# A last tile multiplied by a nested seven-product form: one core, RetNet attention and a SwiGLU block

## The chip, the cores and the metric

The kernel runs on one core of a Trainium2 chip, in float32. The metric is the device time of one execution in microseconds (us). "Before" is the kernel without the change, "after" the kernel with it. Engines are named as in the profile: PE (TensorE), DVE (VectorE), ACT (ScalarE), POOL (GpSimd), SP (SyncE). PSUM banks named bankA, bankB, bankC, bankE, inner and outer are the places that PE writes to.

## The reference

```python
def _attn_ref(q, k, v):                        # 8 x 8 x 576 x 64
    scores = np.matmul(q, k.transpose(0, 1, 3, 2)) / np.sqrt(64)
    gamma = 1.0 - 2.0 ** (-5.0 - np.arange(8))
    rel = pos[:, None] - pos[None, :]
    Dmat = np.where(rel >= 0, gamma[:, None, None] ** rel[None], 0.0)
    return np.matmul(scores * Dmat[None], v)   # no softmax

x = attn.transpose(0, 2, 1, 3).reshape(4608, 512)
g, val = x @ w_gate, x @ w_val                 # 512 -> 1536
out = (g / (1 + np.exp(-g)) * val) @ w_out     # 1536 -> 512
```

The inputs are drawn from normal distributions; nothing in them is sparse.

## The kernel before

**Tiles.** The tokens are worked on in five tiles: tile 0 has 512 tokens and is multiplied in the plain way, tiles 1 to 4 have 1024 each. Every tile has an up stage (x to hidden) and then a down stage (hidden to output). The attention that makes x for a coming tile is cut into "ticks" and mixed among the steps of tiles 1 to 3 (`merge`, L1202); tile 4 has no ticks. The order of all engines' instructions is the order of the program text: each engine has one stream and works through it in order, and so do SP's and ACT's DMA issues, which stand in these streams and wait there for what they need.

**Up stage of tiles 1 to 4.** d_ff is worked on in three quarters of 512 (`NQ` = 3, so named in the code). In each, x (512 x 1024) times the two weight pieces (512 x 512 of gate and value) is computed by a form with 26 products (table `UP`, `N` = 26) in place of the plain number. `up_step` (L1108) is one product: 4 matmuls of 128 x 128 x 256 at L1124 into one bank, two for gate and two for value. `reads` (L1048) then takes the bank away: ACT's copy (L1058), sums with further partial results on DVE or POOL (L1061), and for a finished block ACT's silu (L1145) and the product with the value half (L1148 to L1152), which writes `hid`. Four banks are used in turn, so PE can be four products ahead of what empties them.

**Operands.** The x operands are sums of x blocks (`x_sums`). The weight operands are sums of weight blocks, made once, in tile 1 (`w_sums`, on POOL), and stored to DRAM: `up_ops` on ACT's queue (L1128), `dn_ops` on SP's (L978). From tile 2 on SP fetches them again (L1022) into a ring of eight slots; `fetch()` is called once a step, so the fetch is up to eight steps ahead of its use.

**Down stage.** `down_step` (L1162) is one of 26 products with 6 matmuls (L1173). Its operands are sums of hidden blocks (L1165), its results leave by SP (L1182). In the last four or so steps the first x sums of the next tile are made on DVE.

**Memory.** `arena` holds `hid` (three quarters, 4096 words a partition each), and behind it the up weights of tile 1, whose place later serves as the ring (`ring`). `rest` holds x of the even tiles, partial results (`part`), x sums and hidden sums. `x_odd` holds x of the odd tiles.

Of the kernel before, what the change touches and what calls it, by code (L numbers as in the profile page):

```python
# [12 lines left out]
F32 = mybir.dt.float32  # L13
# [4 lines left out]
ALU = mybir.AluOpType  # L18
# [117 lines left out]

def terms(text):

    return [t.split() for t in text.split(",") if t.strip()]
# [16 lines left out]
def kernel(  # L156
# [83 lines left out]
    ring = arena[:, 4 * QW + 2560 - 8 * 768 :].rearrange("p (s x) -> p s x", x=768)  # L240
# [672 lines left out]
    dn_ops = [dr.tile([P, 768], F32, name=f"dn{i}") for i in range(N)]  # L913

# [96 lines left out]
    fetches = [("dn", 1, i) for i in range(N)]  # L1011
    for n in range(2, NTILE):
        fetches += [("up", qd, i) for qd in range(NQ) for i in range(N)] + [("dn", n, i) for i in range(N)]
    fetched = [0]
    turn = [5, 4, 1, 6, 7, 2, 0, 3]

    def fetch():
        m = fetched[0]
        if m < len(fetches):
            what, a, i = fetches[m]  # L1020
            src = up_ops[a][i] if what == "up" else dn_ops[i]
            nc.sync.dma_start(out=ring[:, turn[m % 8], 0 : src.shape[-1]], in_=src)  # L1022
            fetched[0] += 1

    used = [0]

    def operand():
        m = used[0]
        used[0] += 1
        return ring[:, turn[m % 8]]  # L1030
# [77 lines left out]
    def up_step(n, qd, i):  # L1108
# [5 lines left out]
        if busy:  # L1114
            if i > 1:
                w_sums(qd, i)
            w = up_view(qd)(wslot)
        else:
            w = operand()[:, 0:512].rearrange("p (g x) -> p g x", g=2)
# [7 lines left out]
        if busy:  # L1127
            nc.scalar.dma_start(out=up_ops[qd][i].rearrange("p (g x) -> p g x", g=2), in_=w)  # L1128
            if i in (20, 23) and qd + 1 < NQ:
                first_sums(qd + 1, *((0, 2) if i == 20 else (2, 4)))  # L1130
# [5 lines left out]
            if qd + 1 == NQ:  # L1136
                for _ in range({21: 3, 22: 2, N - 1: 3}.get(i, 0)):
                    fetch()
# [23 lines left out]
    def down_step(n, i):  # L1162
        label, opens, slot, hops, ops = down[i]
        for op in hops:
            add(nc.gpsimd if i % 3 == 1 and op[0] != "nad" else nc.vector, op, hid_view)  # L1165
        w = operand().rearrange("p (q x) -> p q x", q=NQ)
# [30 lines left out]
        if 0 <= at < X_FIRST and n + 1 < NTILE:  # L1197
            x_sums(n + 1, at, at + 2, True)
        go_on(3)


# [91 lines left out]
    for n in range(1, NTILE):  # L1293
        upto = needed(n + 1) if n + 1 < NTILE else done
        cut = (done + upto + (n == 1) * 2) // 2
        ups = [lambda qd=qd, i=i: up_step(n, qd, i) for qd in range(NQ) for i in range(N)]
# [49 lines left out]
```

## Time and profile before

| | before |
|---|---|
| runs, us | 1040.68, 1040.79, 1042.05 (median 1040.79) |
| span of the profiled execution (first to last instruction), us | 1037.2 |
| its own time beside the span | no single time is recorded for it; the median of the runs is 3.6 us above its span |
| mean granted clock of PE | 0.998 |
| busy: PE / DVE / ACT / POOL | 99% / 61% / 29% / 40% of the span |
| DMA | 199.12 MB, mean 192 GB/s |
| last up stage, us from the start | 831.5 to 966.3 |

A row of a profile's group has: source line, engine, operation, output <- inputs with shapes, count, then busy us in all and mean ns of one, then idle us of the engine just before and what ended it. A row of a timeline has: start, length in us, engine, line, operation. PE shows two MATMUL records for each f32 matmul of 128 x 128 x 256, so a step of four matmuls counts as x8.

### The profile page before, as it was taken

The page shows a single profiled execution, that of the slowest core. Times are in us where ns is not written, and L with a number is a line of the kernel's source. Part 1 is how long each engine was busy: PE and PEld are TensorE (multiplying, and loading weights), DVE is VectorE, ACT ScalarE, POOL GpSimd, SP SyncE. Part 2 cuts the span into 40 slices and gives each one's busy share as a digit, 9 for nine tenths or more (in the row PEclk, how much of TensorE's full clock was granted, in tenths as well). Part 3 has the DMA queues.
Part 4 walks back from the last instruction along what each step waited for, and adds up shares of the span by engine and source line. Part 5 has one row for each costly group of instructions (what it writes and reads, how often), then busy time and mean ns, then how long its engine had stood idle before and what let it go on. Part 6 is the DMA issues. An engine that isn't in the chain of part 4 may idle for free.

```text
span 1037.2 us, 21564 instructions
## 1 busy us (share of the span) xinstructions
PE 1023.1 (99%) x8440; PEld 846.0 (82%) x8440; DVE 633.2 (61%) x1070; ACT 299.6 (29%) x653; POOL 419.9 (40%) x369
## 2 busy tenths in 40 slices
PE   6999999999999999999999999999999999999998
PEld 5654555888888888888888888888888888888887
DVE  4488878676768667446458685435465644344644
ACT  3566433253544222222322103223211022231110
POOL 3401265867564236522134057222242583222425
PEclk9999999999999999999999999999999999999999
DMA  9999877777679887674686686555554465555653
GB/s 240 258 279 263 200 218 269 204 205 191 196 194 265 211 244 220 177 197 133 188 231 173 176 208 208 153 142 153 159 171 148 143 196 153 153 153 160 182 163 100
DMA packets 307244, 199.12 MB, mean 192 GB/s; under 512 B 215944, under 2 KB 251784, under 8 KB 307144
## 3 DMA queue, kind: packets, MB, share of 16 engines
q1 hardware_dynamic: 275720, 161.17, 58.2%
q10 hardware_dynamic: 30784, 36.18, 10.4%
q8 instruction: 67, 1.10, 0.5%
q0 software_dynamic: 640, 0.39, 0.2%
q14 instruction: 33, 0.27, 0.1%
HBM read 157.58 MB, written 40.11 MB: 191 GB/s over the span
## 4 chain that ended last, share of the span: by engine, by line
PE 93%; DMA 3%; DVE 1%; ACT 1%; issue 1%; SPq 1%; POOL 0%; DVEq 0%; ACTq 0%; POOLq 0%
PE bankC L1124 13%; PE bankE L1124 13%; PE bankB L1124 13%; PE bankA L1124 13%; PE bankB L1173 7%; PE bankC L1173 7%; PE bankE L1173 7%; PE bankA L1173 7%; PE outer L556 2%; PE bankA L877 2%; PE bankB L877 1%; PE bankE L877 1%; PE outer L583 1%; PE inner L597 1%; PE inner L567 1%; PE bankC L877 1%
## 5 line engine op out<-in xcount | busy, mean ns | idle before, releaser
L1061 POOL TENSOR_TENSOR rest<-rest 128x512 f32<-128x512 f32 x65 | 91.7, 1415 | 234.3 <-DVE rest L1061 212.8
L1145 ACT ACTIVATE io<-rest 128x256 f32<-128x256 f32 x180 | 75.0, 416 | 305.4 <-DVE rest L1061 262.4
L1124 PE MATMUL bankC<-rest,arena 128*128 128x256 f32 x544 | 129.0, 380 | 0.0
L1124 PE MATMUL bankA<-rest,arena 128*128 128x256 f32 x544 | 128.7, 379 | 0.0
L910 POOL TENSOR_TENSOR arena<-arena 128x512 f32<-128x512 f32 (+1 forms) x72 | 110.6, 1549 | 37.3 <-DMA up<-arena 26.5
L1124 PE MATMUL bankB<-rest,arena 128*128 128x256 f32 x512 | 121.2, 380 | 0.5 <-DMA arena<-up 0.5
L1124 PE MATMUL bankE<-rest,arena 128*128 128x256 f32 x512 | 121.4, 380 | 0.1
L1152 POOL TENSOR_TENSOR arena<-rest,io 128x256 f32<-128x256 f32 x72 | 51.9, 726 | 167.7 <-ACT io L1145 167.7
L1124 PEld LDWEIGHTS bankA<-rest,arena 128*128 128x128 f32 x544 | 103.2, 190 | 14.5 <-issue 0.5
L1124 PEld LDWEIGHTS bankC<-rest,arena 128*128 128x128 f32 x544 | 102.9, 190 | 14.4 <-POOL arena L910 0.3
L1124 PEld LDWEIGHTS bankB<-rest,arena 128*128 128x128 f32 x512 | 97.0, 190 | 14.0 <-issue 0.8
L1124 PEld LDWEIGHTS bankE<-rest,arena 128*128 128x128 f32 x512 | 97.0, 190 | 13.7 <-DVE rest L1061 0.5
L910 POOL TENSOR_TENSOR rest<-rest 128x256 f32<-128x256 f32 (+1 forms) x69 | 68.9, 1020 | 71.8 <-DMA dn<-rest 35.3
L1061 DVE TENSOR_TENSOR rest<-bankB,rest 128x512 f32<-128x512 f32 x72 | 48.9, 687 | 67.1 <-PE bankB L1124 52.5
L1061 DVE TENSOR_TENSOR rest<-bankC,rest 128x512 f32<-128x512 f32 x72 | 48.9, 687 | 65.5 <-PE bankC L1124 46.9
L1061 DVE TENSOR_TENSOR rest<-bankA,rest 128x512 f32<-128x512 f32 x72 | 48.9, 687 | 61.2 <-PE bankA L1124 45.1
L1061 DVE TENSOR_TENSOR rest<-bankE,rest 128x512 f32<-128x512 f32 x71 | 48.2, 687 | 60.5 <-PE bankE L1124 47.1
L1148 DVE SCALAR_TENSOR_TENSOR arena<-rest,io 128x256 f32<-128x256 f32 x84 | 56.7, 676 | 10.8 <-ACT io L1145 10.8
L1173 PE MATMUL bankC<-arena 128*128 128x256 f32 x252 | 58.3, 380 | 0.1
L1173 PE MATMUL bankB<-arena 128*128 128x256 f32 x252 | 58.2, 381 | 0.0
L1173 PE MATMUL bankA<-arena 128*128 128x256 f32 x252 | 57.9, 379 | 0.0
L1173 PE MATMUL bankE<-arena 128*128 128x256 f32 x252 | 57.9, 379 | 0.0
(204 smaller groups left out, 1626.1 us busy)
## 6 DMA issues: line engine op xcount, KB each, us to landing
arena<-up SPq DMA_DIRECT2D x234, 256.0 KB, 2.6
arena<-dn SPq DMA_DIRECT2D x104, 384.0 KB, 3.8
up<-arena ACTq DMA_DIRECT2D x78, 256.0 KB, 3.7
dn<-rest SPq DMA_DIRECT2D x78, 128.0 KB, 1.8
out_dram<-rest SPq DMA_DIRECT2D x31, 256.0 KB, 3.9
qk<-in_q_dram SPq DMA_DIRECT2D x108, 72.0 KB, 2.6
qk<-in_k_dram SPq DMA_DIRECT2D x108, 72.0 KB, 2.7
rest<-in_moe_w_out_dram ACTq DMA_DIRECT2D x6, 1024.0 KB
```

The source lines that it names most:

```text
L556: m = nc.tensor.matmul(value(i, hl, c), s["v"][rows, at], ret[rows, c % 2 if whole(i) else hl, c // 2], start=start, stop=start, skip_grou ...
L567: nc.tensor.matmul(z[half[hl], r, c], s["kn"][chunk(i, hl, 2 * c + r)], s["v"][rows, at], start=True, stop=True, skip_group_check=True)
L583: nc.tensor.matmul(xr[half[hl]] if c + 1 == NC else value(i, hl, c), state[half[hl], c, :], s["qT"][half[hl], ts(c, L)], start=False, stop ...
L597: nc.tensor.matmul(sc[chunk(i, hl, 2 * c + r)[0], r if whole(i) else hl, c], kT[half[hl], at], qT[half[hl], at], start=True, stop=True, sk ...
L877: nc.tensor.matmul(bank, w, xs[0][:, c, :], start=(c == 0), stop=(c == HP - 1))
L910: eng.tensor_tensor(out=dst, in0=srcs[0], in1=srcs[1], op=ALU.add if op[0] == "add" else ALU.subtract)
L1061: eng.tensor_tensor(out=at(op[1]), in0=at(op[2]), in1=at(op[3]), op=ALU.add if op[0] == "add" else ALU.subtract)
L1124: m = nc.tensor.matmul(b[:, gv * TB : (gv + 1) * TB], w[:, gv, ts(c, P)], rhs[:, c, :], start=(opens and gv == 0 and c == 0), stop=(c == 1 ...
L1145: nc.scalar.activation(out=s, in_=src[:, 0:TB], func=AF.Silu, scale=-1.0 if negative else 1.0)
L1148: return lambda: nc.vector.scalar_tensor_tensor(out=dst, in0=src[:, TB : 2 * TB], scalar=-1.0, in1=s, op0=ALU.mult, op1=ALU.mult)
L1152: nc.gpsimd.tensor_tensor(out=dst, in0=src[:, TB : 2 * TB], in1=s, op=ALU.mult)
L1173: nc.tensor.matmul(b[:, m * TB : (m + 1) * TB], lhs[:, qd, ts(m, P)], w[:, qd], start=(opens and qd == 0 and m == 0), stop=(qd == NQ - 1), ...
```

## The change

The up stage of the last tile (`FINE = (4,)`) takes another form. A product of a 2 x 2 split matrix by a 2 x 2 split matrix in seven products is applied twice, one inside the other. Per quarter there are 7 outer products (in the order 1, 2, 6, 7, 4, 5, 3), each of 7 inner ones, each with 2 matmuls (gate and value) of 128 x 128 x 256: 98 matmuls a quarter. `fine_up` writes this as steps `step(k, r)`, r from 0 to 6, in the order of inner products 1 of k, 5 of k, 4 of k-1, 6, 2, 3, 7 of k. Six banks are used: three (bankA, bankB, a half of inner) for the chain 1, 6, 7, 4, which is summed up in one bank, three others (bankC, bankE, a half of outer) for 5, 2 and 3. ACT copies four of the results (after 1, 5, 6 and 7) out of the banks; DVE combines them (`made`, `onto`): 3 sums for the first outer product, 7 for the others, 11 for outer product 5. Outer products 2, 4, 5 and 3 finish four blocks each, by ACT's silu and POOL's multiplication (`finish`).

The x sums of this form are four sums of 1024 words on DVE in the down stage of tile 3 (steps 18 to 21), eight of 256 words on POOL after them, and 20 more on POOL in the first steps of the new stage.

The weight operands of the new form, 2 x 6272 words a partition and quarter (`fine_ops` in DRAM), are made in six rounds (`weight_round`), one for each quarter and each of gate and value:

- in the first quarter of the up stages of tiles 2 and 3 (`place_up(0)`, in `hid` of quarters 1 and 2), from step 4;
- in the second quarter of the same stages (`place_up(1)`, in `hid` of quarter 2), from step 0;
- in the down stages of tiles 2 and 3 (`place_down`).

A round loads eight blocks of 128 KB on ACT's queue, negates one on ACT, makes 4 sums of 512, 8 of 256 and 4 of 384 words (DVE and POOL in the up stages, POOL alone in the down stages) and stores 6272 words a partition, again on ACT's queue, 18, 20 and 21 steps after its first (in the down stages in steps 11, 12 and 17). Besides, tile 1 stores three raw blocks of each quarter (`w_raw`, 256 KB each, ACT's queue). In the new stage SP fetches slots of 1792 words, three in turn, with four DMAs for each outer product; elsewhere the fetch works as before.

The core of the diff:

```diff
+FINE = (4,)
+FINE_ORDER = (1, 2, 6, 7, 4, 5, 3)
...
         else:
-            w = operand()[:, 0:512].rearrange("p (g x) -> p g x", g=2)
+            w = operand().rearrange("p (g x) -> p g x", g=2)
+        if n > 1:
+            for f in rounds.pop((n, qd, i), ()):
+                f()
...
             nc.scalar.dma_start(out=up_ops[qd][i].rearrange("p (g x) -> p g x", g=2), in_=w)
+            if i in raw_steps:
+                s = raw_steps[i]
+                nc.scalar.dma_start(out=w_raw[qd][s].rearrange("p (g x) -> p g x", g=2), in_=up_view(qd)(s))
...
+        def up_round(n, stage, qd, g, at):
+            load, turned, outer, z4, z3, store4, store3 = weight_round(qd, g, place_up(stage), (G, V, G) if stage else (V, V, G))
+            for d, blocks in enumerate(((4, 6), (0, 2), (5, 7), (1, 3))):
+                put(n, stage, at + d, lambda blocks=blocks: load(*blocks))
+            put(n, stage, at + 7, turned)
+            for d, f in enumerate(outer):
+                put(n, stage, at + 8 + d, f)
+            for d, f in enumerate(z4[0] + z4[1]):
+                put(n, stage, at + 12 + d // 2, f)
+            for d, f in enumerate(z3):
+                put(n, stage, at + 13 + d, f)
+            put(n, stage, at + 18, lambda: store4(0))
+            put(n, stage, at + 20, lambda: store4(1))
+            put(n, stage, at + 21, store3)
...
+        for n, qd, g in ((2, 0, 0), (3, 1, 1)):
+            up_round(n, 0, qd, g, 4)
+        for n, qd, g in ((2, 0, 1), (3, 2, 0)):
+            up_round(n, 1, qd, g, 0)
+        for n, qd, g in ((2, 1, 0), (3, 2, 1)):
+            down_round(n, qd, g)
...
+        def step(k, r):
+            own, last = 0 <= k < K, 0 < k
+            t = temps(k)
+            if own and r == 0:
+                product(k, 1)
+                nc.scalar.copy(out=t["p1"], in_=bank_of(k, 1))
+            if own and r == 1:
+                product(k, 5)
+                nc.scalar.copy(out=t["p5"], in_=bank_of(k, 5))
+            if last and r == 2:
+                product(k - 1, 4)
+                used[0] += 1
+                fetch()
+            if own and r == 3:
+                product(k, 6)
+                nc.scalar.copy(out=t["u2"], in_=bank_of(k, 6))
+            if own and r == 4:
+                product(k, 2)
+            if own and r == 5:
+                product(k, 3)
+            if own and r == 6:
+                product(k, 7)
+                nc.scalar.copy(out=t["u3"], in_=bank_of(k, 7))
+            if r == 0 and last:
+                done(k - 1, 12)
+            if r == 1 and last:
+                made(k - 1, 22, before["u3"], before["p5"])
+                done(k - 1, 22)
+            if r == 2 and last:
+                onto(k - 1, 21, bank_of(k - 1, 4))
+            if r == 3 and last:
+                done(k - 1, 21)
+            if own and r == 4:
+                made(k, 11, bank_of(k, 2), t["p1"])
+            if own and r == 5:
+                made(k, 12, bank_of(k, 3), t["u2"])
+            if own and r == 6:
+                done(k, 11)
...
-        ups = [lambda qd=qd, i=i: up_step(n, qd, i) for qd in range(NQ) for i in range(N)]
+        ups = fine_up(n) if n in FINE else [lambda qd=qd, i=i: up_step(n, qd, i) for qd in range(NQ) for i in range(N)]
```

## The prediction

> **What bounds the kernel now.** I read the page first, then the up stage of the last tile by itself, then the places where the six weight rounds are put. The engine totals and the chain that ended last:
>
> ```profile
> PE 1023.1 (99%) x8440; PEld 846.0 (82%) x8440; DVE 633.2 (61%) x1070; ACT 299.6 (29%) x653; POOL 419.9 (40%) x369
> ...
> PE 93%; DMA 3%; DVE 1%; ACT 1%; issue 1%; SPq 1%; POOL 0%; DVEq 0%; ACTq 0%; POOLq 0%
> ```
>
> TensorE works 99% of the span and is 93% of the chain, at a granted clock of 0.998. So a product less is worth its full length, and any new wait of PE costs its full length. The stretch table for the last up stage and for tile 3's second quarter (columns: us, then busy time of PE, PEld, DVE, ACT, POOL, granted clock, DMA share, GB/s):
>
> ```profile
> 676.00:700.00 24.00, 24.00 (x238) 21.07 (x237) 10.30 (x20) 4.84 (x11) 5.42 (x6) 1.00 0.51 142
> 831.50:966.30 134.80, 134.80 (x627) 118.65 (x626) 56.87 (x89) 34.41 (x74) 49.79 (x49) 1.00 0.59 165
> ```
>
> PE has no gap there; DVE has 58% of the stage free, DMA about half. PE's timeline gives the price of a product:
>
> ```profile
> 457.12 1.89 PE L1124 MATMUL bankC<-rest,arena 128*128 128x256 f32 x8
> 458.84 1.89 PE L1124 MATMUL bankB<-rest,arena 128*128 128x256 f32 x8
> 460.57 1.89 PE L1124 MATMUL bankE<-rest,arena 128*128 128x256 f32 x8
> ```
>
> A step (4 matmuls, 8 records) starts every 1.727 us: 0.4317 us per matmul.
>
> **The saving.** The old stage has 3 x 26 x 4 = 312 matmuls, the new 3 x 49 x 2 = 294 of the same shape. 18 x 0.4317 = -7.8 us, all on PE's path.
>
> **What the new stage adds.** Per quarter DVE gets 49 combines of 512 words (21 read a bank, 28 only SBUF), ACT 29 copies and 16 silus, POOL 16 multiplies. Groups of the last up stage and two DVE lines of its timeline, without and with POOL at work:
>
> ```profile
> L1152 POOL TENSOR_TENSOR arena<-rest,io 128x256 f32<-128x256 f32 x24 | 17.3, 724 | 52.5 <-ACT io L1145 52.5
> ...
> L1061 DVE TENSOR_TENSOR rest<-bankC,rest 128x512 f32<-128x512 f32 x16 | 10.9, 689 | 16.0 <-PE bankC L1124 15.9
> ...
> L1058 ACT COPY rest<-bankE 128x512 f32<-128x512 f32 x7 | 3.9, 588 | 17.2 <-PE bankE L1124 17.2
> ```
> ```profile
> 613.10 0.68 DVE L910 TENSOR_TENSOR rest<-x_odd 128x512 f32<-128x512 f32 x1
> ...
> 619.10 1.75 DVE L910 TENSOR_TENSOR rest<-x_odd 128x512 f32<-128x512 f32 x1
> ```
>
> Instructions that follow each other start 0.60 us apart on DVE (612.50, 613.10). So 49 cost 29.4 us a quarter; with all 28 SBUF ones at 1.2 us (between 0.68 and 1.75) it is 46 us. PE needs 98 x 0.4317 = 42.3 us. POOL's multiplies fill 16 x 0.72 = 11.6 us of a quarter, so most SBUF combines run beside an idle POOL; I take the low end. The Trainium skill, "SBUF — State Buffer", "Who interferes with whom", says that a DVE instruction with two SBUF inputs and a GpSimd instruction that reads SBUF exclude each other, the later one waiting for the whole of the other. The two lines agree; by the rule alone DVE would wait for at most every multiply once, 29.4 + 11.6 = 41 us, still below PE.
>
> ACT's load (29 x 0.48 + 16 x 0.42 = 21 us) fits. What does not fit is one place: the outer product 5 has 11 combines in place of 7. 11 x 0.6 to 0.73 = 6.6 to 8 us against PE's 6.04 us for seven products. Its last silus come late, ACT's copy of the sixth product of the next outer waits behind them in order, and PE finds that bank full: about 0.6 us, 3 times, +1.9 (0 to 6). Start and drain of the stage: the first down product waits for the last combine, silu and multiply, +0.8 (0.3 to 2). The stage by itself: -7.8 + 1.9 + 0.8 = -5.1 (-7.5 to 0).
>
> **The weight rounds.** Each loads 1 MB, makes 16 sums and stores 6272 words x 4 B x 128 = 3.21 MB through ACT's queue. The sums on DVE and POOL go beside PE: in tile 2's first quad DVE is busy 17.2 of 35 us. The cost is in the DMAs. In the two first quads the stores leave at steps 22, 24 and 25; the second quad begins at step 26 by loading blocks 4 and 6 over the very words that the last two of them read. The load waits, in ACT's own stream, until the stores have landed; behind it stand ACT's copies of the second quarter's first products, which free the four banks. PE can write four banks and stops at step 30.
>
> When do the stores land? Tile 3's throughput in 40 slices of 622 to 700, with 256 KB reads in 2 KB rows alone:
>
> ```profile
> GB/s 297 367 292 354 242 175 142 142 147 145 151 182 158 160 134 134 154 144 143 188 174 146 134 137 155 146 164 170 166 145 140 142 153 154 146 200 24 87 151 162
> ```
>
> The best slice moved 367 GB/s. A 3 KB packet takes 121 ns (median of the trace's packet records): 16 engines make 406. The stores have rows of 3 to 6 KB, so I take the middle, 386; the lowest is 332, the best 5 us with q/k/v loads in it (460 to 465). The weight fetch goes on at 142. So 244 GB/s is left (190 to 264), and 3.21 MB take 13.2 us (12.2 to 16.9).
> The skill's "DMA: Bandwidth & Descriptors", "Issuing engines are not separate DMA queues", says that transfers of all issuing engines run on the same 16 engines and interleave. That speaks against counting on ACT's queue as a way past the fetch; a free second queue would land them at 386 GB/s in 8.3 us, before step 30, and A and B below would be nil.
>
> *A, tile 3.* The stores start near 662.75 (step 22 plus ACT's work ahead of them) and land at 675.95. Loads, then the copy take 1.7 us more; step 30 starts at 674.55 now: +3.1 (2.1 to 6.8). ACT's line there shows how little room there is:
>
> ```profile
> 674.75 0.58 ACT L1058 COPY rest<-bankC 128x512 f32<-128x512 f32 x1 [0.65 <-PE bankC L1124]
> ```
>
> *B, tile 2.* Step 30 is at 455.39 and the stores start at 443.5: they land at 456.7. Here SP also has q, k and v loads ahead of the fetch of quarter 1's product 8:
>
> ```profile
> 456.65 0.55 SPq L317 DMA_DIRECT2D v<-in_v_dram  x1
> 457.29 5.52 SPq L1022 DMA_DIRECT2D arena<-up  x8
> ```
>
> The program hands its eight DMA semaphores in turn to SP's and ACT's transfers, so SP's loads come to wait for ACT's late ones. The fetch leaves about 6.5 us after the stores have landed and takes 3 us; PE needs it at 462.30: 456.7 + 9.5 - 462.3 = +3.9 (2.9 to 7.6), the bank stall included.
>
> *C, quarter 1 to 2 of tile 2.* The second round's stores meet SP's loads (491.7 to 498.8); the next fetch lands 0.3 us before its need now: +1.2 (0 to 3), taken low as only part of a 3 us landing is lost.
>
> *D, the rest.* Tile 1 stores 9 x 256 KB more where DMA share is high, and two down stages give POOL 16 sums each (some 16 us of 67). PE waits 0.5 us for DMA at 427 now; +1.0 (0 to 2). The replaced x sums are about equal work beside PE, at nothing; uncovered it would be 0.7 us each.
>
> Sum: -5.1 + 3.1 + 3.9 + 1.2 + 1.0 = +4.1 us. The profiled execution has a span of 1037.2, the median of runs is 1040.79, so 3.6 lie around the span and stay: 1040.8 + 4.1 = 1044.9. With the ends of the store rate, A and B are 5.0 or 14.4: 1042.9 to 1052.3, and with a stage of -7 and C, D at nothing about 1039.
>
> **Rivals.** A measurement of this kernel can tell 0.2% from no change, 2.1 us.
> 1. *Faster: the stores are out in time.* At 300 GB/s and over, 10.7 us, A is 0.6 and B 1.4; at 386, nil. It decides at about 280 GB/s. Then the fine stage stands alone with C and D: -5.1 + 0 to 2.2: 1035.7 to 1037.9. For it: the ring lies 8 steps ahead, so the fetch may give way for 12 us. Against: loads of q/k/v with 128 and 256 byte packets in tile 2.
> 2. *Slower still: the drain at 190 GB/s.* A 6.8, B 7.6: +11.5, 1052. For it: the 332 GB/s window.
> 3. *DVE bounds the new stage.* At 46 us a quarter it costs 3 x 3.7 = 11.1 in place of 2.7: with the rounds +12.5, 1053. For it: the 1.75 us line; quarter 0 has 20 POOL sums more. Against: POOL is mostly idle in the other two.
> That the stage doesn't shrink is excluded: 18 matmuls are gone from PE's stream.
>
> **How the numbers follow.** Forecast 0.49 (0.02 of it under the bound of faster, 0.12 within 0.2%, 0.35 slower), rival 1 0.28 (0.26 faster, 0.02 within), rival 2 0.15, rival 3 0.08, both slower. Faster 0.28, same 0.14, slower 0.58. The range 1035.7 to 1051.5 leaves out most of rivals 2 and 3. The forecast's own range is 1039 to 1050.
>
> **What would show it.** In the last up stage: 294 matmuls, span near 129.6 us, PE's waits on a bank held by ACT after each outer 5. In tiles 2 and 3 at steps 26 to 30: ACT idle before a load with the stores as releaser, PE waiting for ACT's copies about 3 us, and in tile 2 a PE wait for a fetch. No such wait there would refute A and B (rival 1); DVE without idle time in the last stage would mean rival 3; new PE waits in tile 1 or the down stages would refute D.

## The result, and the profile after

The changed kernel takes 1069.14 us (median of 4 runs, 1066.24 to 1070.89), the kernel before 1040.74 in the same session: a ratio of 1.0265 with a 95% interval of 1.0239 to 1.0290. That is slower by some 28 us, where +4.1 was forecast and the range ended at 1051.5. The profiled execution took 1068.13 us with a span of 1066.4, which is 29.2 more than the span of before.

The engine totals and the chain that ended last, of the changed kernel:

```profile
PE 1028.1 (96%) x8404; PEld 841.2 (79%) x8404; DVE 722.7 (68%) x1166; ACT 331.0 (31%) x719; POOL 502.5 (47%) x454
...
PE 65%; DVE 12%; DMA 10%; POOL 3%; ACT 3%; issue 3%; SPq 2%; ACTq 1%; DVEq 0%; POOLq 0%
```

PE has 36 records less (18 matmuls of two records each), as the change says, but the chain leaves PE for a third of the span. PE's longest waits after the first load of q, which before has too (4.3 us here, 4.6 there); a line says what PE was to write, its line, what it waited for, us in all, times, longest:

```profile
PE bankA L1172 <- DMA arena<-up: 4.2, 1, 4.2
PE bankE L1172 <- ACT rest L1103: 4.0, 1, 4.0
PE bankA L1172 <- DVE rest L1106: 3.0, 2, 2.8
PE inner L1472 <- ACT v L1528: 1.9, 2, 1.5
PE bankB L1472 <- ACT rest L1528: 1.9, 2, 1.5
...
PE bankA L1472 <- ACT rest L1528: 1.4, 1, 1.4
```

L1172 is an up step of tiles 1 to 3, L1472 a product of the new stage. Three kinds of waits in tiles 2 and 3 are each longer than anything PE waited for there before (0.5 us): a fetch that is late, a bank that ACT copies late, a bank that DVE reads late.

To place the loss, the start of every PE step of this execution is set against the same step of before. The difference grows by: 1.0 ahead of tile 1; 1.5 in tile 1; in tile 2, 1.5 at the end of the first quarter, 7.6 in the second, 7.0 in the third, 0 in the down stage; in tile 3, 5.6, 2.7, 0 and 0.7; in the new up stage 0.6; 1.0 in the last down stage. So the tiles that make the weight sums lose some 25 us, and the new stage, which was to win 5.1, wins nothing.

Here is PE's timeline at the start of tile 2's second quarter, then the same stretch with clock and DMA (the seventh number of a row is the granted clock, then DMA share and GB/s):

```profile
457.67 1.89 PE L1172 MATMUL bankB<-rest,arena 128*128 128x256 f32 x8
463.60 3.78 PE L1172 MATMUL bankE<-rest,arena 128*128 128x256 f32 x8 [4.04 <-ACT rest L1103]
467.17 2.98 PE L1172 MATMUL bankC<-rest,arena 128*128 128x256 f32 x8
469.99 1.89 PE L1172 MATMUL bankB<-rest,arena 128*128 128x256 f32 x8
```
```profile
459.30:463.60 4.30, 0.26 (x3) 0.01 (x1) 0.00 (x0) 1.13 (x3) 0.00 (x0) 0.88 0.82 234
463.60:467.40 3.80, 3.80 (x9) 3.08 (x10) 0.00 (x0) 2.42 (x5) 0.00 (x0) 0.50 1.11 263
467.40:470.10 2.70, 2.70 (x9) 2.17 (x9) 0.69 (x1) 0.42 (x1) 1.26 (x1) 0.64 1.18 230
470.10:473.00 2.90, 2.90 (x15) 2.55 (x14) 1.71 (x3) 0.72 (x2) 0.72 (x1) 1.00 1.01 284
```

PE waits 4.04 us, and then two steps take 3.57 and 2.82 us from start to start in place of 1.73, at a granted clock of 0.50 and 0.64. A long wait is paid a second time: of the 7.1 us lost at these steps 4.2 are the wait and 2.9 the clock. What ACT did meanwhile:

```profile
458.70 3.73 ACTq L1275 DMA_DIRECT2D arena<-up  x2
462.47 0.58 ACT L1103 COPY rest<-bankE 128x512 f32<-128x512 f32 x1 [5.95 <-DMA arena<-up]
```

ACT's stream stands in its own DMA issues (the second round's loads) until 462.43, and the copies that free the banks stand behind: the load leaves at 462.10, just after the last store has landed (462.08). This is the bank stall that the forecast named in A and B. The late fetch with which B let the wait end came in time: it landed at 472.88, before PE, late itself by then, reached its product. The new stage, by quarters:

```profile
859.00:903.60 44.60, 43.21 (x197) 36.91 (x196) 35.59 (x45) 20.69 (x41) 31.94 (x38) 1.00 0.55 164
903.60:948.50 44.90, 42.97 (x198) 37.01 (x198) 36.28 (x50) 21.93 (x45) 12.79 (x16) 1.00 0.49 144
948.50:994.30 45.80, 43.20 (x198) 36.79 (x196) 37.14 (x52) 22.34 (x46) 12.96 (x17) 1.00 0.51 152
```

The 294 matmuls take 135.3 us, the 312 of before 134.7. At 0.4317 us a matmul they need 126.9: 8.4 us are waits, in the middle of a stage whose clock is full and whose DMA is half idle. DVE is busy 36 of 45 us.

### The profile page after: what moved, and what is told of

Same layout as the page of the kernel before. It is cut to its first block, busy times and chain, and to the rows that moved or that the text cites. A ratio compares the mean times of both kernels' runs of the same rounds, so it can differ in the third digit from the quotient of the medians.

```text
span 1066.4 us, 21906 instructions
## 1 busy us (share of the span) xinstructions
PE 1028.1 (96%) x8404; PEld 841.2 (79%) x8404; DVE 722.7 (68%) x1166; ACT 331.0 (31%) x719; POOL 502.5 (47%) x454
## 4 chain that ended last, share of the span: by engine, by line
PE 65%; DVE 12%; DMA 10%; POOL 3%; ACT 3%; issue 3%; SPq 2%; ACTq 1%; DVEq 0%; POOLq 0%
PE bankC L1172 7%; PE bankE L1172 6%; PE bankB L1172 6%; PE bankA L1172 6%; PE bankC L1226 6%; PE bankE L1226 5%; PE bankA L1226 5%; PE bankB L1226 5%; DVE rest L1106 3%; DVE rest L1261 2%; PE bankA L1472 2%; DMA fine<-arena 2%; PE inner L1472 2%; PE bankB L1472 2%; PE bankC L1472 1%
## 5 line engine op out<-in xcount | busy, mean ns | idle before, releaser
L1196 ACT ACTIVATE io<-rest 128x256 f32<-128x256 f32 x135 | 55.7, 415 | 234.2 <-DVE rest L1106 180.3
L1172 PE MATMUL bankA<-rest,arena 128*128 128x256 f32 x376 | 91.0, 386 | 8.9 <-DMA arena<-up 4.2
L1172 PE MATMUL bankC<-rest,arena 128*128 128x256 f32 x392 | 95.5, 387 | 1.2 <-DVE arena L1199 0.6
L1172 PE MATMUL bankE<-rest,arena 128*128 128x256 f32 x360 | 87.4, 386 | 4.4 <-ACT rest L1103 4.0
L1172 PEld LDWEIGHTS bankA<-rest,arena 128*128 128x128 f32 x376 | 71.6, 192 | 20.8 <-issue 5.3
L1172 PE MATMUL bankB<-rest,arena 128*128 128x256 f32 x360 | 85.5, 380 | 1.5 <-DMA arena<-up 0.6
L1172 PEld LDWEIGHTS bankC<-rest,arena 128*128 128x128 f32 x392 | 75.4, 194 | 13.9 <-DVE arena L1199 1.0
L1172 PEld LDWEIGHTS bankE<-rest,arena 128*128 128x128 f32 x360 | 69.1, 193 | 14.8 <-ACT rest L1103 4.4
L1172 PEld LDWEIGHTS bankB<-rest,arena 128*128 128x128 f32 x360 | 68.0, 190 | 11.8 <-ACT rest L1103 1.0
L1106 DVE TENSOR_TENSOR rest<-bankC,rest 128x512 f32<-128x512 f32 x57 | 38.7, 687 | 44.4 <-PE bankC L1172 23.2
L1226 PEld LDWEIGHTS bankC<-arena 128*128 128x128 f32 x252 | 47.5, 190 | 8.3 <-issue 1.8
```

The lines of the kernel that those rows point to most:

```text
L1106: eng.tensor_tensor(out=at(op[1]), in0=at(op[2]), in1=at(op[3]), op=ALU.add if op[0] == "add" else ALU.subtract)
L1172: m = nc.tensor.matmul(b[:, gv * TB : (gv + 1) * TB], w[:, gv, ts(c, P)], rhs[:, c, :], start=(opens and gv == 0 and c == 0), stop=(c == 1 ...
L1196: nc.scalar.activation(out=s, in_=src[:, 0:TB], func=AF.Silu, scale=-1.0 if negative else 1.0)
L1226: nc.tensor.matmul(b[:, m * TB : (m + 1) * TB], lhs[:, qd, ts(m, P)], w[:, qd], start=(opens and qd == 0 and m == 0), stop=(qd == NQ - 1), ...
```

## The experiments

The two halves were taken apart first: the new stage without the rounds, and the rounds with the old last stage. "Lag" is the growth of the difference of PE's step starts from the profiled execution of before; "q1 to q3" are the quarters of an up stage. A ratio is to before in the same session. The halves' costs, +0.2% and +2.1%, add up to most of the +2.65% of the whole.

| kernel | us | ratio (95%) | lag tile 2 q1 / q2 / q3 | lag tile 3 q1 / q2 | last up stage |
|---|---|---|---|---|---|
| changed kernel | 1069.1 | 1.0265 (1.0239 to 1.0290) | 1.5 / 7.6 / 7.0 | 5.6 / 2.7 | 135.3 |
| fine_alone | 1041.9 | 1.0021 (1.0000 to 1.0042) | none | none | 135.4 |
| fine_late_silu | 1040.1 | 0.9999 (0.9981 to 1.0017) | none | none | 134.3 |
| fine_no_extra | 1036.4 | 0.9940 (0.9912 to 0.9967) | none | none | 128.4 |
| fine_dve_mult | 1043.4 | 1.0029 (1.0010 to 1.0049) | none | none | 135.8 |
| fine_pool_extra | 1037.8 | 0.9977 (0.9962 to 0.9991) | none | none | 131.1 |
| reorder_full | 1068.0 | 1.0273 (1.0239 to 1.0307) | 1.0 / 6.4 / 3.0 | 6.5 / 2.6 | 137.4 |
| rounds_alone | 1063.3 | 1.0212 (1.0187 to 1.0237) | 1.4 / 7.4 / 2.5 | 4.8 / 2.5 | old |
| rounds_no_store | 1050.9 | 1.0101 (1.0065 to 1.0136) | 0.9 / 2.2 / 0.4 | 4.7 / 0.5 | old |
| rounds_half_store | 1054.8 | 1.0149 (1.0108 to 1.0190) | 0.6 / 6.1 / 0.8 | 6.5 / 0.7 | old |
| rounds_no_second | 1053.7 | 1.0126 (1.0100 to 1.0152) | 0.9 / 6.7 / 0 | 6.9 / 0 | old |
| rounds_down_only | 1041.3 | 1.0013 (0.9995 to 1.0032) | none | none | old |
| rounds_moved | 1064.7 | 1.0214 (1.0175 to 1.0254) | 1.1 / 8.4 / 2.9 | 6.5 / 3.0 | old |
| rounds_pool_store | 1068.9 | 1.0258 (1.0216 to 1.0300) | 2.0 / 8.2 / 7.0 | 3.4 / 6.6 | old |
| rounds_pool_moved | 1067.8 | 1.0279 (1.0241 to 1.0317) | 1.2 / 10.9 / 5.0 | 4.9 / 4.3 | old |
| rounds_pool_sums | 1062.6 | 1.0193 (1.0143 to 1.0243) | 0.7 / 7.2 / 6.4 | 6.9 / 2.7 | old |
| rounds_spread | 1064.1 | 1.0230 (1.0202 to 1.0259) | -0.5 / 7.9 / 4.0 | 3.8 / 6.3 | old |
| rounds_early | 1062.5 | 1.0214 (1.0184 to 1.0244) | 7.0 / 5.6 / 0 | 2.4 / 3.4 | old |
| early_reorder | 1069.7 | 1.0288 (1.0259 to 1.0317) | 6.7 / 5.1 / 0 | 3.2 / 5.1 | 137.4 |

### The new stage by itself

```diff
-    plan_rounds()
...
-                nc.scalar.dma_start(out=w_raw[qd][s]..., in_=up_view(qd)(s))
...
-            src = fine_ops[a][:, g * 6272 : (g + 1) * 6272]
+            src = q.rearrange("b h (s u) d -> (b h s) (u d)", s=2)[:, 1536 * (2 * a + g) : 1536 * (2 * a + g + 1)]
```

> The new last up stage without the six weight rounds and without tile 1's raw stores; its weight operands are read from rows of q, of the same sizes, in place of the sums, so the output is not the reference's. Theory (the stage itself gains nothing: its stalls of 1.7 us after each outer product 5 and 0.6 us after each quarter eat the 7.8 us saved; all the loss comes from the rounds): 1040 to 1043 us, no lag before tile 4, PE waits of 1.7 us three times in the last up stage as in the changed kernel. Rival (the stage stalls only because it follows disturbed tiles or shares DMAs with them): 1034 to 1037 us, the stage near 128 us.

Measured 1041.9, the stage 135.4 us with the same waits at the same products. The theory held: the stage's stalls are its own. DVE's timeline around the end of its first quarter (outer products 5 and 3) and PE's wait there:

```profile
873.01 0.68 DVE L1255 TENSOR_TENSOR v<-bankE,v 128x512 f32<-128x512 f32 x1
873.73 1.23 DVE L1255 TENSOR_TENSOR rest<-v,rest 128x512 f32<-128x512 f32 x1
874.99 0.69 DVE L1255 TENSOR_TENSOR v<-v,arena 128x512 f32<-128x512 f32 x1
```
```profile
873.68 0.73 POOL L1476 TENSOR_TENSOR arena<-v,io 128x256 f32<-128x256 f32 x1 [1.96 <-ACT io L1475]
```
```profile
879.30 1.13 PE L1464 MATMUL bankA<-x_odd,arena 128*128 128x256 f32 x4 [1.39 <-ACT rest L1520]
```

From 871.7 to 886.8 DVE has no gap: 19 combines in 15.2 us, 0.80 each. The 1.23 us one starts 0.05 us after POOL's multiplication. POOL's begins when a silu ends, and that silu began when DVE had finished the sum for it, 0.6 us earlier; DVE, without a gap, is by then at its next sums, most of them of two SBUF operands. So the two meet often, though POOL is mostly idle: in the second and third quarter of the changed kernel's stage (903.6 to 994.3 us) 23 of POOL's 33 multiplications overlap such a combine, 31 of the 57 such combines touch a multiplication (0.98 us on the mean, up to 1.23, against 0.69 for the other 26), and those that read a bank take 0.68 to 0.69 either way.

```diff
                 made(k - 1, 22, before["u3"], before["p5"])
-                done(k - 1, 22)
...
+                done(k - 1, 22)
                 done(k - 1, 21)
```

> As the stage alone, and the silu and multiplication of block 22 of the outer product before are put behind ACT's copy of the sixth inner product (step 3 in place of step 1). Theory (ACT's in-order stream: the copy that frees the chain bank stands behind a silu that waits for DVE's 11 combines): the three waits of 1.7 us shrink to under 0.5 us and the stage is 3 to 5 us shorter than in the stage alone. Rival (DVE itself is late after outer product 5, so that the next bank to be combined is not freed): the waits stay within 0.5 us of what they were, or move to the banks that DVE empties.

The waits before product 7 went (0.1 us left) but others came: 0.4 to 0.5 us before product 3, 1.0 before product 6 of the next outer, 1.95 at the drain. The stage is 1.1 us shorter, not 3 to 5. ACT's order was the last link, not the cause.

```diff
             elif o == 5:
-                combine(nc.vector, r, src, r, 1)
                 combine(nc.vector, at, src, kept(k, c), 1)
```

> As the stage alone, without the four sums that outer product 5 adds to the kept partial results, so it has 7 combines as the others (part of the computation is left out). Theory (DVE's backlog: 18 combines of outer products 5 and 3 take 15 us in the trace where PE needs 12.1): with 14 they take about 12.3, the waits of 1.7 us and of 0.6 us after them go, and the stage is 5 to 7 us shorter than in the stage alone. Rival (the order on ACT, a copy behind a silu, is what PE waits for): the stage is shorter by less than 2 us.

128.4 us: 7.0 shorter, the waits after outer product 5 all gone, only 0.84 before the drain left. Twelve combines a stage (some 7 us of DVE by the forecast's 0.6 each) cost nearly the whole gain, because they stand where DVE already has no time to spare. This settles the stage.

```diff
-            nc.gpsimd.tensor_tensor(out=hid[...], in0=src[:, TB : 2 * TB], in1=s, op=ALU.mult)
+            mults.append(lambda: nc.vector.tensor_tensor(out=dst, in0=src[:, TB : 2 * TB], in1=s, op=ALU.mult))
```

> As the stage alone, with the 16 multiplications a quarter on DVE, a step after their silu, and none on POOL. DVE gets 16 instructions of 256 words more, some 0.35 us each, 5.6 us a quarter. Theory (POOL's multiplication starts with the silu's end, just when DVE combines two operands from SBUF, and each costs that combine 0.55 to 0.65 us, about 9 us a quarter): DVE comes out ahead, the waits after outer product 5 shrink, the stage is 1 to 5 us shorter than the 135.4 us of the stage alone. Rival (the count of DVE's instructions is the limit): the waits grow by 2 us or more a quarter and the stage takes over 139 us.

Neither: 135.8 against 135.4. In the second and third quarter 55 of the 57 combines of two SBUF operands now take 0.69 us, so POOL's multiplications were what lengthened them, but the multiplications cost DVE about as much itself.

```diff
-FINE_ORDER = (1, 2, 6, 7, 4, 5, 3)
+FINE_ORDER = (1, 2, 6, 7, 4, 3, 5)
...
-            elif o == 6:
+            elif o == 6 or o == 3:
                 combine(nc.vector, r, src, r, 1)
...
                 finish(k, c)
+                if seq[k][1] == 5:
+                    finish(k, c, held[spot[c]], (0, 1))
```

> The changed kernel with outer product 3 before 5 in place of after it: 3 is added to the kept sum (7 combines, nothing finished), 5 finishes two blocks at once with 11 combines, and next comes outer product 1 with 3 combines. The sum is the same. Theory (DVE's backlog of 18 combines in two outer products is what PE waits for): the waits after 5 go in quarters one and two, the stage takes 129 to 132 us in place of 135.3, the whole 1062 to 1066 us. Rival (the eight silus and eight multiplications that now follow one outer product take over on ACT and POOL): the stage stays above 134 us.

The rival: 137.4 us. Eight silus now fall on one outer product:

```profile
896.89 1.13 PE L1472 MATMUL outer<-rest,arena 128*128 128x256 f32 x4 [0.55 <-ACT rest L1523]
899.88 2.07 PE L1472 MATMUL bankB<-rest,arena 128*128 128x256 f32 x4 [1.86 <-ACT rest L1530]
```

ACT's copies (L1523, L1530) come late behind pairs of silus, and PE's wait is 1.9 us in place of 1.4. After this wait, and once more later in the stage, PE's granted clock is 0.50 for 3.41 us (899.36 to 902.77, 947.15 to 950.56). That costs at most 1.4 and 1.7 us (half of PE's busy time of 2.89 and 3.41 us there, an estimate), so the clock, and not the silus alone, makes the stage longer than the 135.3; without it some 134.3 would be left, still above the theory's 129 to 132.

```diff
-                combine(nc.vector, r, src, r, 1)
-                combine(nc.vector, at, src, kept(k, c), 1)
+                combine(nc.vector if c == 21 else nc.gpsimd, r, src, r, 1)
+                combine(nc.vector, kept(k, c), src, kept(k, c), 1)
...
-                src = temps(k)[home[c]]
+                src = kept(k, c) if o == 5 else temps(k)[home[c]]
```

> As the stage alone, with three of the four additional sums of outer product 5 on POOL, and the finished block written over the kept one so that the two sums that read the same operand don't wait for each other. DVE has 8 combines after outer product 5 in place of 11, POOL 3 sums of 1.3 us more. Theory (DVE's backlog): the stage is 2 to 5 us shorter than the 135.4 us of the stage alone. Rival (POOL's sums block DVE's combines of two SBUF operands, or the multiplications behind them come late): within 1.5 us of it or longer.

131.1 us, 4.3 shorter than the stage alone and 3.6 shorter than the old stage, by handing three sums of outer product 5 to POOL and writing the finished block over the kept one; what the second alone is worth was not measured. DVE and POOL of the whole stage (third and fifth busy time, 109.1 and 57.7 us before this edit):

```profile
834.20:965.30 131.10, 129.02 (x590) 110.96 (x589) 104.67 (x136) 64.89 (x132) 75.34 (x80) 1.00 0.53 158
```

### The rounds by themselves

```diff
-FINE = (4,)
+FINE = ()
```

> The six weight rounds and tile 1's raw stores as in the changed kernel, and the last tile in the form of before (nothing of the rounds is used). Theory: the whole of the loss is here, 1066 to 1070 us, with the same lags at the same steps of tiles 2 and 3 (7 us at steps 4 to 6 of the second and of the third quarter of tile 2, 5 us at steps 22 to 24 of tile 3's first quarter). Rival (the two halves of the change disturb each other): under 1060 us.

1063.3 us, below the 1066 to 1070 expected; the lags are at the places named, but 2.5 us in tile 2's third quarter in place of 7. There the size differs from kernel to kernel with the same program text at that place (2.5 here, 3.0 in reorder_full, 7.0 in the changed kernel).

```diff
-            nc.scalar.dma_start(out=to[:, 1024 * n : 1024 * (n + 1)], in_=raw_flat[...])
...
-            nc.scalar.dma_start(out=to[:, 3584:5120], in_=mid)
```
(all stores of the rounds)

> As the rounds alone, with loads and sums, but the sums are not stored (19 MB less to DRAM). Theory (ACT's and SP's streams stand behind stores that have not landed): the lags at the starts of the second and third quarters go, 15 to 19 us of the loss with the lowered clock after them; the 5 to 7 us at the ends of the first quarters stay, since they come from the sums on DVE: 1047 to 1052 us. Rival (the sums, not the stores, are the cost): over 1058 us.

1050.9: the stores are half of the loss, and the 4.7 us at the end of tile 3's first quarter stay. The total is as expected; but 12.4 us went and not the 15 to 19 named, as 2.2 us stay in tile 2's second quarter.

```diff
-            f = [flat[2][:, 768 * i : 768 * (i + 1)] for i in range(2)]
-            last3 = flat[2][:, 1536:2688]
+            f = [flat[2][:, 1408 + 768 * i : 1408 + 768 * (i + 1)] for i in range(2)]
+            last3 = flat[2][:, 2944:4096]
```

> As the rounds alone, with the fresh sums of the first quads' rounds 1408 words further on in hid's third quarter: the blocks 4, 0, 2, 1 and 3 that the second round loads no longer lie over words whose store is under way, blocks 5 to 7 only over those of the first store, at step 22. Theory (the load waits for the stores' landing because of the same words, in front of ACT's copies): the lag at steps 30 to 32 (7 us in tile 2, 2 us in tile 3) shrinks below 2 us, 1054 to 1058 us. Rival (the eight DMA semaphores handed round between SP's and ACT's queues make ACT's next DMA wait for a transfer eight before it, whatever its words): the lag stays within 2 us, 1061 to 1065 us.

No gain: 1064.7. The chain of waits there, and ACT and PE in the timeline:

```profile
454.15 7.77 DMA qk<-in_q_dram
...
467.92 4.11 DMA arena<-up
```
```profile
462.31 0.59 ACT L1103 COPY rest<-bankC 128x512 f32<-128x512 f32 x1 [2.76 <-DMA qk<-in_q_dram]
```
```profile
472.16 3.65 PE L1172 MATMUL bankC<-rest,arena 128*128 128x256 f32 x8 [3.26 <-DMA arena<-up]
```

ACT now waits for one of SP's q loads, with which its load shares no word; what they share is the semaphore (the program gives eight to the two queues in turn). The q load takes 7.8 us to land, and SP's k and v loads and the fetch behind them leave late. So "the same words" of the forecast's step A does hold the load in the changed kernel, where it leaves 0.02 us after the last store has landed (462.10 after 462.08, 699.20 after 699.18); but without the shared words another wait takes its place at the same steps, and in tile 3 2.3 us are lost there in place of the 2.0 of rounds_alone.

```diff
-            nc.scalar.dma_start(out=to[...], in_=...)
+            nc.gpsimd.dma_start(out=to[...], in_=...)
```
(all stores of the rounds)

> As the rounds alone, with the rounds' 3.2 MB stores issued on POOL's queue in place of ACT's. Theory (the cost of the stores is that ACT's and SP's streams stand behind them, not the bytes): the lags at the third quarter of tile 2 go (2 to 7 us), the one at steps 30 to 32 stays in part, as ACT's load still waits for the same words: 1052 to 1060 us. Rival (the bytes are the cost): within 3 us of the rounds alone, 1060 to 1066 us. A third outcome, that POOL's work of issuing them delays its products, would show as new waits for POOL.

1068.9, above both ranges and no better than rounds_alone (the intervals of the two ratios overlap). PE has no new waits for POOL from 400 to 800 us, so the third outcome does not show either. The rows agree with the rule weighed in the forecast, that the issuing engine doesn't make a separate path.

Both of these edits together:

> As the rounds alone, with both: stores on POOL's queue, and the fresh sums moved 1408 words so that the next loads mostly do not lie over words under way. Either edit by itself changed nothing (1064.7 and 1068.9 us). Theory (two waits stand one behind the other, for the same words and for a semaphore shared between the queues, and each alone is enough): the lag at steps 30 to 34 of tile 2 and of tile 3 falls below half, to 3 us and 1 us, 1053 to 1060 us. Rival (the bytes: loads, stores and fetches together want more than the 16 engines move in that time, whatever waits for what): within 3 us of 1064.

1067.8. The stores share neither words nor, on POOL's queue, a semaphore with the transfers of ACT and SP (one load in ACT's stream still waits for words, 1.3 us at most), and the fetch is late all the same. The chain, and the stretch:

```profile
450.68 10.21 DMA qk<-in_q_dram
...
466.27 3.49 DMA arena<-up
469.89 3.75 PE bankC L1172 x8
```
```profile
455.00:461.00 6.00, 4.27 (x20) 3.42 (x18) 1.38 (x2) 2.68 (x6) 1.26 (x1) 1.00 1.09 341
```

One q load takes 10.2 us to land beside the stores, while the DMA engines are busy all the time (a share of 1.09, as the view counts it); in the kernel before, the q loads of that stretch took 2.1 (median). The rival, the transfers themselves, fits; the theory that the two waits are all falls. SP's and ACT's loads still share semaphores here.

```diff
-            nc.scalar.dma_start(out=to[:, 3584:5120], in_=mid)
+            nc.scalar.dma_start(out=to[:, 3584 : 3584 + 768], in_=half(mid))
```
(and so for each store)

> As the rounds alone, with the same number of stores in the same places on ACT's queue, each of half its words (the other half of the sums is not stored). If the wait is for the landing and the landing takes bytes through a shared rate: half the bytes land about 6 us earlier, and most of the lag at steps 30 to 32 and at the third quarter of tile 2 goes, 1052 to 1057 us. If it is the number of transfers and their turn on the semaphores: within 3 us of the rounds alone, 1060 to 1066 us.

1054.8: with the same count and order and half the bytes, in rows half as long, 15.0 us over before in place of 23.2 (by the lags of the profiled executions from tile 2 on, 15.4 in place of 19.3). The total is the one expected of the bytes; the place is so only in part: tile 2's third quarter and tile 3's second are nearly free, but in tile 2's second 6.1 us stay, 5.1 of them at steps 34 to 36, where PE waits for a fetch that left behind slow q loads (5.1 and 4.1 us).

```diff
-        for n, qd, g in ((2, 0, 1), (3, 2, 0)):
-            up_round(n, 1, qd, g, 0)
```

> As the rounds alone, without the two rounds in the second quads (four rounds are left: two in first quads, two in down stages; the other sums are not made). Theory now (in tile 2 the first round's 3.2 MB of stores, the second round's loads, the q, k and v loads and the fetch want the 16 engines at once, so each in turn is late): the lag at steps 30 to 34 of tile 2 falls to about half, 3 to 4 us, since the stores and the q, k, v loads stay; none at tile 2's third quarter; 5 us at the end of tile 3's first quarter stay (sums): 1049 to 1054 us. Rival (only ACT's loads standing behind the stores cost time): no lag at steps 30 to 34 at all, 1045 to 1048 us.

1053.7. Without any second round 6.7 us stay in tile 2's second quarter, where the theory left 3 to 4, so the stores and SP's loads collide without it; the rival (only ACT's loads behind the stores) falls. In tile 3, where SP has no such loads at that time, nothing is left there.

```diff
-            ... (G, V, G) if stage else (V, V, G))
+            ... (G, V, G) if stage else (G, G, G))
```

> As the rounds alone, with all 16 sums of the first quads' rounds on POOL instead of 12 on DVE. Theory (DVE empties the banks late because the sums stand ahead of its reads in its own stream): the lag at steps 22 to 25 of tile 3's first quarter (4.8 us) and of tile 2's (1.4 us) goes, PE's wait there for DVE with it: 1056 to 1060 us. Rival (DVE is slow because POOL's instructions on SBUF stand in its way, so that moving the sums changes who waits): the lag stays above 3 us.

At steps 22 and 23 of tile 3's first quarter 5.3 us are lost, not less. The wait changed hands:

```profile
679.10 0.69 DVE L1106 TENSOR_TENSOR rest<-bankA,rest 128x512 f32<-128x512 f32 x1 [5.22 <-POOL rest L1106]
```
```profile
671.00 6.85 POOL L1261 TENSOR_TENSOR arena<-arena 128x256 f32<-128x256 f32 x8
```

DVE reads the bank late because the partial result that it adds comes from POOL, which does eight weight sums first.

```diff
-                put(n, stage, at + 12 + d // 2, f)
+                put(n, stage, at + 10 + d, f)
```
(and the others two steps earlier)

> As the rounds alone, with the same sums on the same engines spread over more steps: outer sums two steps earlier, the eight of 256 words one a step (16 steps' length in all instead of 10). Theory (at steps 16 to 21 the sums, the products and the reads of the banks come together, and DVE and POOL have spare time before and after): the wait of 2.8 us at step 22 of tile 3's first quarter and the slow clock after it (4.7 us together) fall below 1.5 us, 1056 to 1061 us. Rival (it is the amount, not the crowding): still over 3.5 us there.

At step 22 of tile 3's first quarter 1.2 us are left, as expected: it was crowding (2.6 us that came at its steps 4 and 5 make up the 3.8). But the whole is 1064.1: the second quarter's lag rose from 2.5 to 6.3. PE came there earlier (step 26 starts at 686.1 us, in rounds_alone at 688.5), and the stores did not: ACT's copy behind them starts at 695.45 and 695.42. One stall had hidden a part of the next.

```diff
-            put(n, stage, at + 18, lambda: store4(0))
-            put(n, stage, at + 20, lambda: store4(1))
-            put(n, stage, at + 21, store3)
+            put(n, stage, at + 14, lambda: store4(0))
+            put(n, stage, at + 18, lambda: store4(1))
+            put(n, stage, at + 18, store3)
```
(besides the spread sums, the first quads' rounds from step 1)

> As the rounds alone, with the first quads' rounds three steps earlier, the sums one a step, and the stores as soon as their sums are made: steps 15 and 19 in place of 22, 24 and 25 in the first quads, 14 and 18 in place of 18, 20 and 21 in the second. Theory (the bytes need about 13 us of the engines before step 30): the stores have landed by step 26, the lags at steps 30 to 34 and at the third quarter of tile 2 fall below 3 us each, the crowding at step 22 below 2 us: 1047 to 1055 us. Rival (the total of bytes in tile 2 is too much wherever it lies): 1060 to 1066 us.

1062.5. The lags at steps 30 to 34 (0.7 us) and in the third quarter (0) shrank, but 7.7 us came at step 16 of tile 2's first quarter and 4.9 at steps 22 to 24 of its second, where PE waits 3.1 us for DVE and then has the low clock. SP's waits (425 to 520) and the chain there:

```profile
SPq L1052 <- DMA fine<-arena: 8.7, 3, 7.5
```
```profile
432.96 2.63 DMA fine<-arena
...
435.65 2.52 DMA arena<-up
...
438.31 3.75 PE bankC L1172 x8
```

SP's fetch of weights waits 7.5 us for a store of ACT's, which itself waited for a sum on DVE. They share a semaphore and no word. So the turn of the semaphores costs too: it ties SP's fetch to DVE's lateness.

The edits of rounds_early and of reorder_full in the whole kernel:

> Both at once in the whole kernel, early stores and outer product 3 before 5: 1042 to 1051 us if both theories hold. Not expected to beat the kernel before (1040): the sums of the rounds still cost some 5 us and the stage at best wins 5.

1069.7, where 1042 to 1051 was expected: the costs of both halves are there again, 6.7 us in tile 2's first quarter and a stage of 137.4 us.

```diff
-        for n, qd, g in ((2, 0, 0), (3, 1, 1)):
-            up_round(n, 0, qd, g, 4)
```
(besides the second rounds)

> As the rounds alone, with only the two rounds in the down stages of tiles 2 and 3 left, and tile 1's raw stores. Theory (a round costs where SP's loads of q, k and v, DVE's and POOL's work and the next loads meet; a down stage has time for 16 POOL sums and 3.2 MB): 1040 to 1042.5 us, the 0.7 us at step 10 of tile 3's down stage. Rival (every 3.2 MB stored costs its 4 to 6 us wherever it lies): 1048 to 1052 us.

1041.3, within the interval of no change; lag 0.7 us in tile 3's down stage and none elsewhere. A round is not dear in itself: 16 sums and 3.2 MB fit into a down stage.

## Why the prediction was wrong

The direction and the places of A, B and C were right, the sum was not. The profiled execution grew by 29.2 us, 25.1 more than forecast: 16.9 of these lie in tiles 2 and 3 (25.1 there, where A, B and C had 8.2), 5.7 in the last up stage (+0.6 in place of -5.1) and 2.5 elsewhere. By the prediction's steps:

- **Saving, -7.8.** Right: with the backlog away the stage takes 128.4 us.
- **Stalls of the stage, 1.9 + 0.8.** They were 8.4. The step that failed is "most SBUF combines run beside an idle POOL; I take the low end". POOL is idle 72% of the second and third quarters, but 31 of the 57 SBUF combines there touch one of its multiplications, because a multiplication starts soon after a sum of DVE, when DVE is mostly at its next ones. The share of busy time said nothing on that. The two DVE lines quoted for the price (613.10 and 619.10) are not of the last up stage, and the 1.75 stands beside POOL sums of 512 words, not beside multiplications. And the stall was priced as if each outer product began without debt: 11 x 0.6 to 0.73 against 6.04. The 7 combines of the next one don't win it back: 19 in 15.2 us against PE's 12.1 for two outer products, a debt of some 3 us (an estimate from these rows). The third rival (DVE bounds the stage, 11.1 us of waits) was nearer to the 8.4 than the forecast's 2.7, and got a chance of 0.08; its sign, DVE without idle time, did not show (36 of 45 us busy): DVE is short only after outer product 5. The Trainium skill's "SBUF — State Buffer", "Who interferes with whom", had the mechanism; the trace's number for it is 1.23 us for 0.69.
- **Sums "beside PE", at nothing.** They cost 1.3 us in tile 2 and 4.7 in tile 3 (steps 22 to 24), 1.8 of that by the low clock. DVE was busy 17.2 of 35 us on the mean, but eight sums of 256 words, four of 384, the products and the bank reads fell into some six steps. No cover was named for those steps.
- **A, +3.1.** 2.2 measured, in its range, 2.7 with the end of the quarter. The cause named (the words) is what the load waits for, but rounds_moved shows that it does not decide: without it another wait costs as much.
- **B, +3.9.** 7.1. The wait of 4.2 is near the number, but by luck: it was for a bank behind ACT's stream, not for the fetch, on which the number was built. The low clock after it, 2.9, was in no term.
- **C, +1.2.** 7.0 in the changed kernel, 2.5 in rounds_alone and 3.0 in reorder_full. It was "taken low as only part of a 3 us landing is lost". In the trace ACT's stream stands 8.4 us behind stores of its own, the q, k and v loads follow, and PE waits 4.2 us for a fetch; 1.8 more are the low clock.
- **D, +1.0.** 0.7 in the down stage. Ahead of tile 2 the difference to before reaches 6 us in executions without any round and falls to -1.7 in one with them, so nothing there can be put down to the raw stores.
- **The store rate.** It was right for the stores themselves: the last one landed 13.0 us (tile 2) and 13.6 us (tile 3) after the first had left, and 13.2 was forecast. What failed is that it was applied to the stores alone, and what the stores do to loads of 128 and 256 byte packets was left out: a q load that took 2.1 us took 7.8 in the changed kernel and 10.2 in rounds_pool_moved.

The mechanism of the loss in tiles 2 and 3 is shown in so far as half the bytes take 4 to 8 us away and no bytes 10 to 12 (lags and medians); that one place lost can turn up at the next is shown by rounds_spread and rounds_early. How the rest divides between transfers that land slowly and the turn of the semaphores stays open: the first was seen in rounds_pool_moved, the second in rounds_early, but no run has neither. Why tile 2's third quarter varies so is settled in part: in the changed kernel the clock was halved after the wait there (1.8 us), in rounds_alone it was not; why the wait is 2.3 us in one and 4.2 in the other is open.

No version that computes the whole beat the kernel before. The new stage with its sums on POOL would, by 0.2% (0.09% to 0.38%), but with its weight sums left out; two rounds in down stages cost next to nothing, and no such place was tried for the four others.

## What to carry to other kernels

An engine that is 58% idle can still be late: count its instructions over the few steps where they come together, with the price that they have when the other engine works too, and carry the debt into the next step. Work off the critical path that moves megabytes is priced at its place, by what else wants the queues and semaphores there, and a wait of PE by its length and by the slow clock after it. When one stall hides the next, mending it alone shows nothing.

## What the runs showed of the hardware

PE's granted clock is 1.00 or 0.50 in the trace's clock records; 0.64 and 0.88 above are means over both. It stays at 0.50 for 3.41 us or twice that, and such a stretch starts a whole number of 3.41 us after another, not where a wait ends. In the changed kernel 462.54 to 469.37, 520.57 to 523.98 and 684.41 to 687.82 are such stretches; the last:

```profile
684.41:687.82 3.41, 3.41 (x10) 2.70 (x9) 1.57 (x3) 1.25 (x3) 2.04 (x3) 0.50 0.44 124
```

They cost some 6.5 us: 2.9 and 1.8 in tile 2, 1.8 in tile 3. In all runs of this case no wait of PE up to 1.84 us was followed by the low clock and every one of 3.21 us and over was. Between these it came after some (1.86 us in reorder_full, 2.76 in the changed kernel) and not after others (2.27 in rounds_alone, 3.16 in rounds_early). The Trainium skill's "TensorE: Matmul & The Clock Gate", "Part 1: The HAM clock gate (the "warmup" mystery)", states that an idle window of about 3.4 us, which runs freely, halves the clock. The rows agree with the half, the length and the fixed grid; but waits shorter than the window, 1.86 and 2.76 us, lowered the clock here, so the measurement decides. How much of a window has to be idle is not shown.

A q load of 72 KB, 2.1 us to landing before, took up to 10.2 us beside 3.2 MB of stores.
